# A fused spectral filter and gated FFN: one norm placed first on VectorE, five constants on GpSimd, a fold scratch in another tile

## The chip, the cores and the metric

The kernel runs on one core of a Trainium2 chip. The metric is the device time of one execution in microseconds. Engines are named as in the profile: PE is TensorE (PEld its weight loads), DVE is VectorE, ACT is ScalarE, POOL is GpSimd, SP is SyncE, which here only issues transfers.

## The reference

```
xn = layernorm(x)                                     # over D, eps 1e-5
X  = rfft2(xn, axes=(S, D)) * (w_r + 1j * w_i)
s  = irfft2(X, s=(S, D)).astype(bfloat16)
h  = (gelu(xn @ w_gate) * (xn @ w_up)) @ w_down       # tanh form of gelu
out = x + s * silu(h)
```

x is [1, 2048, 640] in bfloat16; the filters are [2048, 321]; the FFN has 640 inputs and 1536 hidden columns.

## The kernel before

**Tiling.** The 2048 rows are dealt into 16 slabs of 128 rows (slab n1 holds the rows n1, n1 + 16, ...). X holds all of them, [128, 16, 640]. Four slabs make a group of the FFN: normalized rows are transposed into xnT[g] (640 columns in 5 chunks of 128, by 512 rows); 12 hidden tiles each take a gate product (5 matmuls into a bank psg), a gelu on ScalarE (ge, line 799), an up product (5 matmuls into a bank psu) and a product of the two on VectorE (uT, line 801), which empties the bank. There are two banks of each name. Then come 12 matmuls for each output half (line 820), and the silu (lines 825 to 829).

**The FFT.** Its two axes are done by matmuls with sine tables that the kernel makes itself: integer phases (vt, ft_v, vg), a mask on VectorE, sines on ScalarE, some by transposing transfers. The tables Tinv and Tfwd are built from vt in the scratch tile GEN; FT and FI from fv; MG and its turned forms N1 and N2 from vg. The row axis is prepared by folds: VectorE adds and subtracts mirrored column blocks of four slabs at once (fold_x, fold_a, fold_b, then fold_y, lines 471 to 521), nine instructions for a set of four slabs. Their results f and y feed the matmuls pz (slab_S1, line 549), ScalarE copies those out, pd follows (slab_D), and the spectrum goes through DRAM (ZDR) into the tile B2. Then come the filter product with W1 and W2 (line 644), the way back through DRAM (UDR), the inverse matmuls (pv, pd at line 559), and the final product with the silu and sum with x (lines 770 and 771, x read again by load_xt, line 700).

**Scratch for the folds.** fold_x, fold_a and fold_y write to a scratch that overlays ftm and vt in GEN (scratch, line 464). So the folds of slabs 0 to 3 have to come after the sine that reads vt (tinv_sin, line 343). W2 is loaded with w_i much later (w_minus, w_plus, w_twin with index 1) and holds nothing until then.

**What sets the order.** The order is written out by hand. `back` (line 861) lists pieces of the FFN in turn; behind piece s the items of `plan[s]` run, put there by `put`. Each engine executes its instructions in program order; semaphores hold it where a buffer or an operand isn't ready. The places around the change: the first entry of `back` (slab 0's gate and up tiles, with slab 1's norm, in two parts, and its transposes between them), place 1 (inv_rest: six VectorE instructions for the pair i_r and o_r, read by ft_v of index 9 at place 12), places 17 to 23 (statistics of slabs 8 to 12), places 24 to 27 (folds of slabs 0 to 3), places 28 to 33 (folds of 4 to 7, with mg_mask at 30). A norm needs three steps: statistics on VectorE (lines 179 and 185), a power on GpSimd (line 197, its result rst), and the scaling on VectorE (line 208).

Of the kernel before, what the change touches and what calls it, by code (L numbers as in the profile page):

```python
# [10 lines left out]
BF16 = mybir.dt.bfloat16  # L11
INT32 = mybir.dt.int32
ACT = mybir.ActivationFunctionType
ALU = mybir.AluOpType
P = 128
S = 2048
D = 640
# [15 lines left out]
def kernel(  # L33
# [40 lines left out]
    with tc.manual_schedule():  # L74
        build(nc, locals())


def build(nc, env):
    consts, big, wts, xg, work, psA, psB = (env[k] for k in ("consts", "big", "wts", "xg", "work", "psA", "psB"))
    ZDR, UDR, X, Wg, Wu, Wd, W1, W2 = (env[k] for k in ("ZDR", "UDR", "X", "Wg", "Wu", "Wd", "W1", "W2"))  # L80
    xv, outv, wgv, wuv = (env[k] for k in ("xv", "outv", "wgv", "wuv"))
# [63 lines left out]
    GEN = big.tile([P, NH * L // 2], INT32, tag="sB", name="GEN")  # L145
# [17 lines left out]
    def c1(name, dt=FP32):  # L163
        return consts.tile([P, 1], dt, name=name)
# [75 lines left out]
    scr = goff[0]  # L240
# [7 lines left out]
    def bits(name, fields):  # L248
        n = len(fields)
        ti = consts.tile([P, n], INT32, name=name + "i")  # L250
        tf = consts.tile([P, n], FP32, name=name)
        for k, (shift, mask) in enumerate(fields):
            nc.vector.tensor_scalar(out=ti[:, k:k + 1], in0=pint, scalar1=shift, scalar2=mask,
                                    op0=ALU.logical_shift_right, op1=ALU.bitwise_and)
        nc.vector.tensor_copy(out=tf, in_=ti)
        return [tf[:, k:k + 1] for k in range(n)]

    def affine(name, src, a, b):
        t = c1(name)
        nc.vector.tensor_scalar(out=t, in0=src, scalar1=float(a), scalar2=float(b), op0=ALU.mult, op1=ALU.add)  # L260
        return t

    kh_f, hi_f, s_f, h_f, pf, n1_f, z_f = bits(
        "pb", [(1, 31), (6, 1), (0, 31), (5, 1), (0, 127), (1, 15), (0, 1)])
# [4 lines left out]
    def fma(name, src, k, add, dt=FP32):  # L269
        t = c1(name, dt)  # L270
        nc.vector.scalar_tensor_tensor(out=t, in0=src, scalar=float(k), in1=add, op0=ALU.mult, op1=ALU.add)
        return t
# [8 lines left out]
    def times(name, src, k, by):  # L281
        t = c1(name)
        nc.vector.scalar_tensor_tensor(out=t, in0=src, scalar=k, in1=by, op0=ALU.mult, op1=ALU.mult)
        return t
# [29 lines left out]

    def inv_rest():
        cq, hk = kc
        l_s = affine("l_s", s_f, 2.0, 256.0)
        l_k = fma("l_k", h_f, 2.0, l_s)
        l_r = fma("l_r", times("lh", hk, 1.0, hi_f), 1.0, l_k)
        i_r = affine("i_r", l_r, 2.0, 0.0)  # L320
        o_r = fma("o_r", l_r, 1.0, cq)
        ab.append((i_r, o_r))

    fwd_consts()
# [136 lines left out]

    y0s = {}

    def scratch(o, n, w):
        return GEN[:, scr + o:scr + o + n * w // 2].bitcast(BF16).rearrange("p (s d) -> p s d", s=n)

    def slabs(n0, n):
        assert all(("n", n0 + k) in done for k in range(n))
        return X[:, n0:n0 + n, :]

    def fold_y(n0, n, k):
        xn = slabs(n0, n)
        t = scratch(2304, n, 256)
        if k == 0:
            nc.vector.tensor_tensor(out=t, in0=xn[:, :, 0:256], in1=xn[:, :, 256:512], op=ALU.add)
            return
        if k == 1:
            y = work.tile([P, 4, P], BF16, tag="y0", bufs=2, name="y0")
            for a in range(n):
                y0s[n0 + a] = y[:, a, :]  # L480
            y0s[n0, n] = y = y[:, 0:n, :]
            nc.vector.tensor_tensor(out=y, in0=t[:, :, 0:P], in1=t[:, :, P:256], op=ALU.add)
            return
        y = y0s[n0, n]
        nc.vector.tensor_tensor(out=y, in0=y, in1=xn[:, :, 512:640], op=ALU.add)

    def fold_x(n0, n, k):
        xn = slabs(n0, n)
        xp = scratch(0, n, D)

        def blocks(t):
            return t.rearrange("p s (t e) -> p s t e", e=64)

        def outer(t):
            return t.rearrange("p s (t b e) -> p t s b e", b=2, e=64)[:, 0:5:2]

        ref = blocks(xn)[:, :, 2:8:5, :]
        if k == 0:
            nc.vector.tensor_tensor(out=outer(xp), in0=outer(xn),
                                    in1=ref.unsqueeze(1).to_broadcast([P, 3, n, 2, 64]), op=ALU.subtract)  # L500
        else:
            nc.vector.tensor_tensor(out=blocks(xp)[:, :, 6:2:-3, :], in0=blocks(xn)[:, :, 6:2:-3, :], in1=ref,
                                    op=ALU.subtract)

    def fold_a(n0, n, k):
        xp, uvt = scratch(0, n, D), scratch(1280, n, 512)
        lo = xp[:, :, 0:384].rearrange("p s (t e) -> p s t e", e=192)[:, :, :, 0:P]
        hi = xp[:, :, 256:640].rearrange("p s (t e) -> p s t e", e=192)[:, :, :, 64:192]
        nc.vector.tensor_tensor(out=uvt[:, :, 256 * k:256 * k + 256].rearrange("p s (t e) -> p s t e", e=P),  # L509
                                in0=lo, in1=hi, op=(ALU.add, ALU.subtract)[k])  # L510

    def fold_b(n0, n, k):
        if k == 0:
            f = work.tile([P, 4, 512], BF16, tag="xf", bufs=2, name="f")
            for a in range(n):
                xf[n0 + a] = f[:, a, :]
            xf[n0, n] = f[:, 0:n, :]
        s4 = scratch(1280, n, 512).rearrange("p s (w d) -> p s w d", w=2)
        dm = xf[n0, n].rearrange("p k (g d) -> p k g d", g=4)
        gs, op = ((slice(0, 4, 3), ALU.add), (slice(1, 3), ALU.subtract))[k]  # L520
        nc.vector.tensor_tensor(out=dm[:, :, gs, :], in0=s4[:, :, :, 0:P], in1=s4[:, :, :, 255:127:-1], op=op)  # L521
# [178 lines left out]
    def load_xt(pair):  # L700
        t = work.tile([P, 4, 512], BF16, tag="xf", bufs=2, name="xt")
        t = t.rearrange("p a b -> p (a b)")[:, 0:2 * D].rearrange("p (a d) -> p a d", a=2)
        for a in range(2):
            xts[2 * pair + a] = t[:, a, :]
        nc.sync.dma_start(out=t, in_=xv[:, 2 * pair:2 * pair + 2, :])

    def slab_S1i(n1):
        V = st_c["V"][n1]
# [128 lines left out]
    GG, UU = ((0, 0), (1, 0), (2, 0)), ((0, 1), (1, 1), (2, 1))  # L837
# [11 lines left out]
    def slab_Tparts(n1):  # L849
# [3 lines left out]
        for (a, b), ev in zip(PARTS, evs[::-1] if n1 == 0 else evs):  # L853
            pt = psB.tile([P, 5, P], BF16, tag="b")
            for c in range(a, b):
# [2 lines left out]
        done.add(("T", n1))  # L858

    NP = 8  # L860
    back = [(run, (ffn_slab, 0, GG + UU[:1]), (norm_parts, 1), (vt_iota, 1), (ffn_slab, 0, UU[1:2]),
             (slab_Tparts, 1), (ffn_slab, 0, UU[2:]), (bn_half, 2, 0)),
            (run, (ffn_slab, 1, GG[:2]), (bn_half, 2, 1), (ffn_slab, 1, UU[:1] + GG[2:] + UU[1:2]), (bn_join, 2),
             (root, 2, 1), (ffn_slab, 1, UU[2:]), (norm, 2))]
# [12 lines left out]
    def put(s, *item):  # L877
        plan[s].append(item)

    back.insert(2, (run,))  # L880
    plan.append([])
    put(1, inv_rest)
    put(2, bn_half, 3, 0)
    put(3, bn_half, 3, 1)
# [33 lines left out]
    put(31, mg_sin)  # L918
    put(31, mg_build)
    for at, *items in (  # L920
            (17, (stats, 8)), (18, (stats, 9)), (20, (stats, 10)), (22, (stats, 11), (root, 8, 4)), (23, (stats, 12)),
            (24, (fold_x, 0, 4, 0), (fold_x, 0, 4, 1)), (25, (fold_a, 0, 4, 0), (fold_a, 0, 4, 1)),
            (26, (fold_b, 0, 4, 0), (fold_b, 0, 4, 1)), (27, (fold_y, 0, 4, 0), (fold_y, 0, 4, 1), (fold_y, 0, 4, 2)),
            (28, (fold_x, 4, 4, 0)), (29, (fold_x, 4, 4, 1)), (30, (fold_a, 4, 4, 0)),
            (31, (fold_a, 4, 4, 1), (fold_b, 4, 4, 0)), (32, (fold_b, 4, 4, 1), (fold_y, 4, 4, 0)),
            (33, (fold_y, 4, 4, 1), (fold_y, 4, 4, 2), (norm, 8)), (34, (norm, 9), (norm, 10), (norm, 11)),
            (35, (stats, 13)), (36, (stats, 14), (stats, 15)),
            (37, (root, 12, 4), (fold_x, 8, 4, 0), (fold_x, 8, 4, 1)), (38, (fold_a, 8, 4, 0)),
            (39, (fold_a, 8, 4, 1), (fold_b, 8, 4, 0)), (40, (fold_b, 8, 4, 1)),
            (41, (fold_y, 8, 4, 0), (fold_y, 8, 4, 1)), (42, (fold_y, 8, 4, 2), (norm, 12)),  # L930
            (43, (norm, 13), (norm, 14), (norm, 15)), (44, (fold_x, 12, 4, 0)),
            (45, (fold_x, 12, 4, 1), (fold_a, 12, 4, 0)), (46, (fold_a, 12, 4, 1)),
            (47, (fold_b, 12, 4, 0), (fold_b, 12, 4, 1)), (48, (fold_y, 12, 4, 0)),
            (49, (fold_y, 12, 4, 1), (fold_y, 12, 4, 2))):
        for it in items:
            put(at, *it)
# [31 lines left out]
    for i, at in enumerate((vs0 - 1, vs0, vs0 + 6, vs0 + 15, vs0 + 24)):  # L968
        put(at, gather, i)
    put(vs0 - 2, load_xt, 0)  # L970
    put(vs0 + 4, load_xt, 1)
    for i, (n0, n) in enumerate(DG):
        a = vs0 + 7 * i
        for k in range(n):
            put(a + (2 * k if n == 3 else 1), slab_S1i, n0 + k)
        d = a + 6 if n == 3 else a + 3
# [55 lines left out]
```

## Time and profile before

| what | value |
|---|---|
| median of 3 runs | 201.37 us (201.34 to 201.65) |
| profiled execution | 201.39 us |
| its span, first to last instruction | 199.6 us |
| mean granted TensorE clock | 0.997 |
| DMA | 32.43 MB, mean 163 GB/s |

The span and the busy times are those of the one profiled execution; 1.79 us of its time lie around the span. A row of a timeline has the start in us, the busy time in us, the engine, the line, the operation, out<-in with shapes, and the number of instructions merged into the row; a bracket gives the idle time of the engine before the row and what ended it. A row of several matmuls ends when the last one leaves the pipeline, about 0.165 us after the next row can start, so rows overlap. In a row of transfers come the count, the size and the time from issue to landing. Lines of the page that end in percentages by engine are the chain of work that ended last, followed back from the last instruction.

### The profile page before, as it was taken

What the parts mean: (1) busy time and instruction counts of PE and PEld (TensorE: products, weight loads), DVE (VectorE), ACT (ScalarE), POOL (GpSimd) and SP (SyncE); (2) the same over time, 40 slices, a digit from 0 to 9 for tenths busy, and PEclk for the clock granted to TensorE, in tenths of its full rate; (3) what the DMA queues carried; (4) which work ended last, traced back from release to release, by engine and by line L of the source; (5) the groups of instructions that cost most, each with busy time, mean ns of one, the idle gap of its engine ahead of it and who ended that gap; (6) DMA issues with size and microseconds to landing.
All of it is one profiled execution on the core that took longest, in us unless ns stands there. A gap on an engine that the chain in (4) does not pass through costs nothing.

```text
span 199.6 us, 4145 instructions
## 1 busy us (share of the span) xinstructions
PE 192.4 (96%) x1533; PEld 118.3 (59%) x1548; DVE 131.7 (66%) x321; ACT 124.3 (62%) x219; POOL 37.8 (19%) x63
## 2 busy tenths in 40 slices
PE   7899999999999999999999999999999999999993
PEld 4688854767555555576543333457765555557772
DVE  7787869999899832223666556433349786977673
ACT  4567657966976677634788687523474747376631
POOL 4317869989030110000000000000000000000000
PEclk9999999999999999999999999999999999999998
DMA  5999997364575693329972022359700416142521
GB/s 174 328 364 371 371 291 163 82 206 171 154 152 149 143 321 90 113 66 298 259 203 99 5 99 102 132 130 274 258 0 34 135 36 194 36 131 42 192 79 55
DMA packets 37044, 32.43 MB, mean 163 GB/s; under 512 B 13088, under 2 KB 34976, under 8 KB 36768
## 3 DMA queue, kind: packets, MB, share of 16 engines
q1 hardware_dynamic: 36928, 30.86, 52.7%
q0 software_dynamic: 96, 1.31, 1.7%
q8 instruction: 12, 0.20, 0.4%
q14 instruction: 8, 0.07, 0.1%
HBM read 19.03 MB, written 7.88 MB: 135 GB/s over the span
## 4 chain that ended last, share of the span: by engine, by line
PE 87%; DVE 5%; ACT 4%; issue 1%; DMA 1%; POOL 0%; DVEq 0%
PE psg L795 25%; PE psu L795 25%; PE psu L820 11%; PE psg L820 11%; PE pv L712 2%; PE pd L559 2%; PE pu L659 2%; PE pd L580 2%; PE pz L549 2%; PE px L632 2%; DMA X<-in_A_x_dram 1%; PE pd L563 1%; DVE GEN L509 1%; DVE f L521 1%; DVE st L179 1%
## 5 line engine op out<-in xcount | busy, mean ns | idle before, releaser
L795 PE MATMUL psg<-xnT,Wg 128*128 128x512 bf16 (+2 forms) x287 | 60.5, 338 | 1.0 <-ACT xnT L857 0.2
L795 PE MATMUL psu<-xnT,Wu 128*128 128x512 bf16 (+2 forms) x288 | 60.7, 339 | 0.5 <-issue 0.2
L801 DVE TENSOR_TENSOR uT<-psu,ge 128x512 bf16<-128x512 f32 (+2 forms) x59 | 34.5, 586 | 26.7 <-PE psu L795 22.8
L820 PEld LDWEIGHTS <-uT 128*128 128x128 bf16 x396 | 37.3, 98 | 14.0 <-issue 0.4
L799 ACT ACTIVATE ge<-psg 128x512 bf16<-128x512 f32 (+2 forms) x59 | 30.5, 517 | 23.0 <-PE psg L795 22.1
L795 PEld LDWEIGHTS <-Wu 128*128 128x128 bf16 x295 | 26.9, 98 | 24.1 <-issue 2.5
L795 PEld LDWEIGHTS <-Wg 128*128 128x128 bf16 x295 | 26.6, 98 | 21.2 <-issue 2.3
L820 PE MATMUL psg<-Wd,uT 128*128 128x320 bf16 (+1 forms) x204 | 30.7, 295 | 0.0
L820 PE MATMUL psu<-Wd,uT 128*128 128x320 bf16 (+1 forms) x192 | 28.7, 296 | 0.0
L644 DVE TENSOR_TENSOR X<-xs,W 128x972 bf16<-128x972 bf16 (+2 forms) x22 | 13.3, 649 | 10.2 <-ACT xs L640 9.2
L585 ACT CAST zd<-pd 128x660 bf16<-128x660 f32 x16 | 11.3, 707 | 9.6 <-PE pd L582 8.8
L714 ACT CAST W<-pv 128x640 bf16<-128x640 f32 x16 | 11.1, 696 | 5.0 <-PE pv L712 5.0
L179 DVE BATCH_NORM_STATS2 st<-X 128x6 f32<-128x320 bf16 x32 | 14.0, 477 | 0.2 <-DMA X<-in_A_x_dram 0.2
L737 ACT ACTIVATE W<-pd 128x960 bf16<-128x960 f32 (+2 forms) x14 | 10.1, 780 | 5.6 <-PE pd L563 5.5
L665 ACT CAST X<-pu 128x486 bf16<-128x486 f32 (+4 forms) x22 | 12.3, 558 | 0.3
L640 ACT CAST xs<-px 128x972 bf16<-128x972 f32 (+2 forms) x11 | 10.3, 937 | 2.9 <-PE px L632 2.9
L551 ACT CAST GEN<-pz 128x640 bf16<-128x640 f32 x16 | 11.2, 700 | 1.3 <-PE pz L549 1.3
L829 DVE SCALAR_TENSOR_TENSOR G<-th,psg 128x320 bf16<-128x320 f32 x8 | 3.9, 488 | 12.2 <-ACT th L828 12.2
L743 DVE TENSOR_TENSOR W<-W 128x960 bf16<-128x960 bf16 (+1 forms) x12 | 6.9, 599 | 3.9 <-ACT W L737 3.8
L770 DVE TENSOR_TENSOR Yall<-Yall,G 128x640 bf16<-128x640 bf16 (+3 forms) x19 | 8.3, 435 | 1.6 <-ACT G L825 1.3
L771 DVE TENSOR_TENSOR Yall<-Yall,xt 128x640 bf16<-128x640 bf16 (+3 forms) x19 | 8.3, 439 | 0.7
L197 POOL TENSOR_TENSOR rst<-ve,mhalf 128x1 f32<-128x1 f32 (+1 forms) x6 | 5.6, 929 | 14.7 <-DVE ve L195 14.7
(139 smaller groups left out, 208.4 us busy)
## 6 DMA issues: line engine op xcount, KB each, us to landing
ZDR<-zd SPq DMA_DIRECT2D x32, 80.2 KB, 2.6
xt<-in_A_x_dram SPq DMA_DIRECT2D x8, 320.0 KB, 3.7
UDR<-X SPq DMA_DIRECT2D x10, 240.8 KB, 2.4
out_dram<-Yall SPq DMA_DIRECT2D x14, 160.0 KB, 2.1
B<-ZDR SPq DMA_DIRECT2D x8, 240.8 KB, 4.2
W<-UDR SPq DMA_DIRECT2D x4, 481.5 KB, 6.7
X<-in_A_x_dram SPq DMA_DIRECT2D x3, 640.0 KB, 10.8
Wd<-in_B_w_down_dram SPq DMA_DIRECT2D x1, 1920.0 KB, 14.2
```

Of the source, the lines that this page charges most:

```text
L179: nc.vector.bn_stats(out=st_n[n1][:, k, :], in_=X[:, n1, 320 * k:320 * k + 320])
L551: nc.scalar.copy(out=Zt[n1], in_=pz)
L585: nc.scalar.copy(out=zd.rearrange("p c (q e) -> p c q e", e=10), in_=pd[:, :, 0:330].rearrange("p c (e q) -> p c q e", q=33))
L640: nc.scalar.copy(out=xs, in_=px[:, :, 0:n * w].rearrange("p k (h l) -> p k h l", l=w))
L644: nc.vector.tensor_tensor(out=pp[-1], in0=xs, in1=WT[:, :, h0:h0 + n, l0:l0 + w], op=ALU.mult)
L665: nc.scalar.copy(out=us[:, :, :, c0:c0 + (w + 1 - m) // 2], in_=pv[:, :, :, m:w:2])
L714: nc.scalar.copy(out=vs, in_=pv)
L737: nc.scalar.activation(out=eo[:, b, :, a0:a1].rearrange("p k a n -> p a k n"), in_=py[b][:, a0:a1], func=ACT.Copy, scale=(2.0 if silu[a0] ...
L795: nc.tensor.matmul(ps, lhsT=WT[:, c, t * P:(t + 1) * P], rhs=xnT[g][:, c, c0:c1_], start=(c == 0), stop=(c == 4))
L799: nc.scalar.activation(out=ges[t], in_=ps, func=ACT.Gelu_apprx_tanh)
L801: nc.vector.tensor_tensor(out=uT[g][:, t, c0:c1_], in0=ps, in1=ges[t], op=ALU.mult)
L820: nc.tensor.matmul(ph, lhsT=uT[g][:, t, j * P:(j + 1) * P], rhs=Wd[:, t, c0:c1_], start=(t == 0), stop=(t == NT - 1))
```

## The change

It does five things. In the first entry of `back`, slab 1's norm (two VectorE instructions, and the small memset ahead of an iota) moves from behind slab 0's first up tile to ahead of it in program order; TensorE's order is the same, and on VectorE the norm now precedes the first two products uT. The constants of inv_rest are made by five instructions on GpSimd (one multiplies by hi_f and adds in one step) in place of six on VectorE; they stand on GpSimd between the powers of slabs 2 and 3. The scratch of the folds of slabs 0 to 3 lies in W2. The statistics of slabs 8 to 12 are put at places 16, 17, 18, 20 and 22 instead of 17, 18, 20, 22 and 23; on VectorE those of slabs 8 and 12 now precede a uT product that they followed. The loads of x for pairs 0 and 1 are issued one slab at a time.

```diff
     def inv_rest():
         cq, hk = kc
-        l_s = affine("l_s", s_f, 2.0, 256.0)
-        l_k = fma("l_k", h_f, 2.0, l_s)
-        l_r = fma("l_r", times("lh", hk, 1.0, hi_f), 1.0, l_k)
-        i_r = affine("i_r", l_r, 2.0, 0.0)
-        o_r = fma("o_r", l_r, 1.0, cq)
+        l_s, l_k, l_r, i_r, o_r = (c1(n) for n in ("l_s", "l_k", "l_r", "i_r", "o_r"))
+        for out, in0, s1, s2 in ((l_s, s_f, 2.0, 256.0), (l_k, h_f, 2.0, l_s), (l_r, hk, hi_f, l_k),
+                                 (i_r, l_r, 2.0, 0.0), (o_r, l_r, 1.0, cq)):
+            nc.gpsimd.tensor_scalar(out=out, in0=in0, scalar1=s1, scalar2=s2, op0=ALU.mult, op1=ALU.add)
         ab.append((i_r, o_r))
...
-    def scratch(o, n, w):
-        return GEN[:, scr + o:scr + o + n * w // 2].bitcast(BF16).rearrange("p (s d) -> p s d", s=n)
+    def scratch(n0, o, n, w):
+        if n0 == 0:
+            t = W2.rearrange("p a h l -> p (a h l)")[:, 2 * o:2 * o + n * w]
+        else:
+            t = GEN[:, scr + o:scr + o + n * w // 2].bitcast(BF16)
+        return t.rearrange("p (s d) -> p s d", s=n)
...
-        nc.sync.dma_start(out=t, in_=xv[:, 2 * pair:2 * pair + 2, :])
+        w = 1 if pair < 2 else 2
+        for a in range(0, 2, w):
+            nc.sync.dma_start(out=t[:, a:a + w, :], in_=xv[:, 2 * pair + a:2 * pair + a + w, :])
...
-    back = [(run, (ffn_slab, 0, GG + UU[:1]), (norm_parts, 1), (vt_iota, 1), (ffn_slab, 0, UU[1:2]),
+    back = [(run, (ffn_slab, 0, GG), (norm_parts, 1), (vt_iota, 1), (ffn_slab, 0, UU[:2]),
              (slab_Tparts, 1), (ffn_slab, 0, UU[2:]), (bn_half, 2, 0)),
...
-            (17, (stats, 8)), (18, (stats, 9)), (20, (stats, 10)), (22, (stats, 11), (root, 8, 4)), (23, (stats, 12)),
+            (16, (stats, 8)), (17, (stats, 9)), (18, (stats, 10)), (20, (stats, 11), (root, 8, 4)), (22, (stats, 12)),
```

The calls of scratch in fold_x, fold_a, fold_b and fold_y pass n0 as well.

## The prediction

> **What bounds the kernel now.** I read the page first: its busy line, then the chain of work that ended last, then the timelines of TensorE, VectorE, GpSimd and ScalarE around the edits.
>
> ```profile
> PE 192.4 (96%) x1533; PEld 118.3 (59%) x1548; DVE 131.7 (66%) x321; ACT 124.3 (62%) x219; POOL 37.8 (19%) x63
> PE 87%; DVE 5%; ACT 4%; issue 1%; DMA 1%; POOL 0%; DVEq 0%
> ```
>
> TensorE is busy for 96% of the span, and the change adds and removes no matmul: in the built kernels its instructions stand in the same order. So the time moves only by TensorE's idle stretches. I take the start of a group plus the number of its matmuls times their pitch (0.054 us for 128 columns, 0.109 for 256, 0.216 for 512, 0.136 for 320, all start to start in the timeline) and compare it with the start of the next. From 9.3 us on the groups touch, apart from a few tenths here and there (some, as at 58.2 us, are only a missing record). The stretches that an edit can reach are these:
>
> ```profile
> 7.20 0.72 PE L795 MATMUL psu<-xnT,Wu 128*128 128x128 bf16 x10
> 8.39 0.54 PE L856 MATMUL pt<-ident,X 128*128 128x128 bf16 x5 [0.47 <-DVE X L208]
> ...
> 13.49 0.71 PE L795 MATMUL psg<-xnT,Wg 128*128 128x256 bf16 x5
> 14.29 0.71 PE L795 MATMUL psu<-xnT,Wu 128*128 128x256 bf16 x5
> 14.84 0.71 PE L795 MATMUL psg<-xnT,Wg 128*128 128x256 bf16 x5
> 15.47 0.71 PE L795 MATMUL psu<-xnT,Wu 128*128 128x256 bf16 x5
> 16.24 0.45 PE L537 MATMUL pt<-ident,X 128*128 128x128 bf16 x5
> ```
>
> Idle: 7.75 to 8.39 (0.64, slab 1's norm), 9.04 to 9.30 (0.26, copies of slab 1's transposes), 14.04 to 14.29 (0.25) and 15.39 to 15.47 (0.08), both for a bank that VectorE empties late, and 16.02 to 16.24 (0.22, slab 3's norm). A last one lies at 42.82 to 43.11 (0.29): the matmul of the first y waits for the last fold.
>
> **Part 1, slab 1's norm ahead of two evictions.**
>
> ```profile
> 6.98 0.58 POOL L197 TENSOR_TENSOR rst<-ve,mhalf 128x1 f32<-128x1 f32 x1 [3.09 <-DVE ve L195]
> ...
> 7.76 0.29 DVE L801 TENSOR_TENSOR uT<-psu,ge 128x128 bf16<-128x128 f32 x1 [0.86 <-ACT ge L799]
> 7.96 0.63 DVE L208 TENSOR_SCALAR X<-X,mva,rst 128x384 bf16<-128x384 bf16 x2
> ```
>
> The factor is ready at 7.56, but VectorE sits on the eviction of the first up tile until 7.76, and the norm starts at 7.96. With the norm first it starts 0.04 behind the factor (so far apart are 12.25 and 12.29 at slab 2), at 7.60: 0.36 sooner. The two evictions follow at 8.16 and 8.36 instead of 7.76 and 8.52. Behind them the third up piece waits for a bank, free at 8.45 plus 0.04; the transposes end at 8.41, so that wait is 0.08, but it is hidden: the next matmuls wait anyway for slab 1's copies. ScalarE's moves from 8.77 to 8.41 with the transposes; VectorE's can start at 8.61 (it started at 8.97) since the second eviction leaves it at 8.56. Both end 0.36 sooner. **Gain 0.36**, and 9.30 becomes 8.94.
>
> **Part 2, five constants from VectorE to GpSimd.** VectorE spends 12.65 to 13.43 on six small instructions (l_s to o_r), 0.78, ahead of a half statistic and the eviction of 13.83. Everything there moves 0.36 with part 1; without the six the eviction starts at 12.69 (norm of slab 2 at 11.93, 0.36 to the half statistic, 0.40 to the eviction), 1.14 sooner. Its bank is free at 13.14, and TensorE comes for it at 13.68: the 0.25 goes, and so the 0.08 (next bank free at 14.3, wanted at 14.77). Slab 3's factor is asked for at 14.04 (15.15 less 1.11 to 1.14), the norm runs 14.62 to 15.07 and its transposes can start at 15.13. TensorE, 0.69 ahead by now, arrives at 15.34, so the 0.22 goes too. **Gain 0.55.** What is late next: the weights. The row for the third up block says 7.9 us from an issue at 5.54, so it lands at 13.44, and TensorE now wants it at 13.68: 0.24 of cover.
>
> ```profile
> Wu<-in_B_w_up_dram SPq DMA_DIRECT2D x1, 480.0 KB, 7.9
> ```
>
> GpSimd's five constants are new, and stand between the factors of slabs 2 and 3. The nearest rows are its scalar instructions of 128x1 between 33.61 and 36.21: ten starts in 2.60 us, 0.26 each; with waits on one another up to 0.35. That is 1.3 to 1.75 us behind 11.89, over at 13.2 to 13.6; the factor is asked for at 14.04. The largest row of that shape (46.39, beside folds) has 0.62: 3.1 us, done at 14.99, 0.95 late, less 0.21 of cover at the transposes: 0.74 lost. The low end is nothing, since the constants are not read before 23 us. I take nothing, because the rows beside statistics and evictions are the nearest to what VectorE does there.
>
> **Part 3, statistics of slabs 8 to 12 sooner, folds of 0 to 3 in another tile.**
>
> ```profile
> 36.12 2.17 ACT L345 ACTIVATE Tinv<-GEN,negpi 128x1024 bf16<-128x1024 int32 x2
> ...
> 37.36 0.96 DVE L499 TENSOR_TENSOR GEN<-X 128x1536 bf16<-128x1536 bf16 x1 [0.16 <-ACT Tinv L345]
> ...
> 42.59 0.46 DVE L485 TENSOR_TENSOR y<-y,X 128x512 bf16<-128x512 bf16 x1
> ```
>
> The folds overwrite the phases that the sine reads, so they wait for it; they take 5.70, and y is ready at 43.06. In W2 they wait for VectorE alone. I ran its new order forward with all starts 0.91 sooner: eviction 8 at 28.45 (its gelu ends then), statistics 9 and 10, eviction 9 at 31.1, statistic 11, eviction 10 at 32.9, statistic 12, eviction 11 at 34.58 to 35.25, folds 35.2 to 40.9. TensorE wants y at 41.9, so 1.0 is spare: **gain 0.29**. The statistics read loads that landed at 21.4 and 29.2, before their new places (26.7 and 33.5). Eviction 11 is now behind statistic 12; its reader is the twelfth matmul of the first down group, at 35.57, so 0.3 remains. The loads of w_i into W2 now wait for the folds: SyncE issues the first at 47.96, less 1.2, long after 40.9. Nothing is queued up there.
>
> Folds 4 to 7 stay in the old tile; the sine is done at 37.4 and they start at 40.8, so they don't wait. But the mask of vg, third on VectorE among them, waits for GpSimd's eight vg steps:
>
> ```profile
> 37.06 0.37 POOL L384 TENSOR_SCALAR vg<-kr,n1x,phm 128x16 int32<-128x16 int32 x1
> 37.40 1.42 POOL L384 TENSOR_SCALAR vg<-kr,n1x,phs 128x16 int32<-128x16 int32 x1
> ```
>
> Such a step takes 0.37 until the folds begin and 1.42 beside the first of them. Now all eight, from 35.5 on, meet folds. VectorE reaches the mask at 42.0; by then at least four are done, and with VectorE waiting the rest take 0.37 to 0.5 each, so the mask ends at 43.0 to 44.2. ScalarE wants it at 43.24 and has nothing else until 44.36 (0.72 idle before 45.55 in its timeline), the instruction itself 0.40. Cost 0 to 0.3; I take 0, as folds of 4 to 7 have 5 us until their matmul at 53.06. The Trainium skill ("SBUF — State Buffer", section "SBUF: two separate sides") says that a VectorE instruction with two SBUF inputs and a GpSimd instruction lock a shared port pair for a whole instruction, the later one fully blocked. The trace agrees (0.37 against 1.42); by that rule this edit costs GpSimd some 4 us more beside folds, and the sum stays, or loses the 0.3.
>
> **The xt loads** of pairs 0 and 1 become four issues instead of two, 0.4 us more each on SyncE's queue, which is idle from 139.4 to 152.88; first read at about 150. Nothing.
>
> **Sum.** 0.36 + 0.55 + 0.29 = 1.20. The profiled execution took 201.39 (span 199.6 and 1.79 around it), 0.02 above the median of 201.37. 201.39 - 1.20 = 200.19; I predict **200.2**. Behind 43 us TensorE has the same work in the same order and its suppliers move with it.
>
> **The rivals.** (a) The forecast, 0.60, itself between 200.0 and 200.4. (b) The weights become the bound in the head: with a landing some 0.5 later than the row, the 0.24 of cover is gone and 0.3 lost, 200.5. For it: the loads run at 358 GB/s through that stretch; against: the row itself. 0.12. (c) The last fold still ends late or the mask holds ScalarE: the 0.29 stays, 200.5; against it 1.0 of cover. 0.10. (d) Slower: GpSimd's constants. One mechanism, between the factors of slabs 2 and 3. Free for the five are 14.04 + 0.21 - 11.89 = 2.36 us, 0.47 each. Above 3.56, 0.71 each, the gain is eaten; at 1.42 each (vg beside folds) they take 7.1, slab 3's transposes wait 4.7, and 204.9 results. For it: factor and norm wait in GpSimd's order; against: no two-input fold runs there. 0.08, with the milder 0.74 loss (200.9) at its edge. (e) The change does not do what it says: TensorE finds the banks and copies just as late through another wait, 201.4. The idle stretches have VectorE's rows right ahead of them, so 0.10.
>
> **Numbers.** A measurement here can tell about 0.2%, 0.4 us. Faster by more (below 200.97): a, b, c, 0.82; within: e, 0.10; slower: d, 0.08. Range 199.8 to 201.0: it holds a to c with the bound of the constants (200.9), and 0.2 below the lowest term for what I may not have seen.
>
> **What would show it.** Right: the norm of slab 1 starts at 7.6 and slab 1's first gate matmul near 8.95; no idle on TensorE at its fifth up tile or slab 3's transposes, which start near 15.3; y's matmul directly behind its f group, folds from 35.2. Wrong: a weight load of Wu ending later than TensorE's arrival at 13.7, five long GpSimd rows behind 11.9, a ScalarE wait for the mask near 43.5, or new idle behind 50 us.

## The result, and the profile after

The changed kernel takes **201.04 us** (median of 9 runs, 200.58 to 201.59) against 201.47 (9 runs, 201.34 to 201.72) for the kernel before in the same measurement: a ratio of 0.9976 with a 95% interval from 0.9965 to 0.9987. It is faster, by 0.43 us and not by the 1.2 that were forecast, and lies just outside the range. The profiled execution took 201.11 (span 199.3), against 201.39 (199.6).

So there are two questions: did the terms of the sum come, and if so, where did they go? First the stretches of TensorE that the prediction named, in the timeline of the changed kernel:

```profile
7.40 0.72 PE L800 MATMUL psu<-xnT,Wu 128*128 128x128 bf16 x10
8.39 0.54 PE L861 MATMUL pt<-ident,X 128*128 128x128 bf16 x5 [0.26 <-DVE X L208]
8.85 0.44 PE L800 MATMUL psu<-xnT,Wu 128*128 128x128 bf16 x5
9.30 0.72 PE L800 MATMUL psg<-xnT,Wg 128*128 128x128 bf16 x10
...
13.49 0.71 PE L800 MATMUL psg<-xnT,Wg 128*128 128x256 bf16 x5
14.03 0.71 PE L800 MATMUL psu<-xnT,Wu 128*128 128x256 bf16 x5
14.58 0.71 PE L800 MATMUL psg<-xnT,Wg 128*128 128x256 bf16 x5
15.12 0.71 PE L800 MATMUL psu<-xnT,Wu 128*128 128x256 bf16 x5
15.67 0.44 PE L540 MATMUL pt<-ident,X 128*128 128x128 bf16 x5
```

From 13.49 to 15.67 each group starts 0.54 or 0.55 behind the one before, which is its own length: the idle stretches of before (0.25, 0.08, 0.22) are gone. At 8.39 a wait for slab 1's norm is still there (0.26 instead of 0.47), and slab 1's first gate matmul starts at 9.30, as before, not at 8.94. The first y follows its f group at once:

```profile
42.01 0.39 PE L552 MATMUL pz<-Tfwd,f 128*128 128x128 bf16 x4
42.24 0.22 PE L552 MATMUL pz<-Tfwd,y 128*128 128x128 bf16 x1
```

The lead lasts. TensorE's last group of the down product starts at 194.44, against 195.31 in before, and VectorE's last instruction ends at 196.11, against 196.97: 0.86 sooner. But the span is only 0.3 shorter. From VectorE's last end to the end of the span before took 2.63 and the changed kernel takes 3.19. I call this stretch **the tail**; the spans are printed to 0.1, so a tail is good to some 0.05. These are VectorE's last instruction and SyncE's last issue, first before, then after:

```profile
196.74 0.23 DVE L771 TENSOR_TENSOR Yall<-Yall,xt 128x128 bf16<-128x128 bf16 x1
197.00 0.33 SPq L772 DMA_DIRECT2D out_dram<-Yall  x1
```

```profile
195.88 0.23 DVE L776 TENSOR_TENSOR Yall<-Yall,xt 128x128 bf16<-128x128 bf16 x1
196.35 0.33 SPq L777 DMA_DIRECT2D out_dram<-Yall  x1
```

Before, the last output transfer is issued 0.03 behind VectorE's end; after, 0.24 behind. And it takes longer to land. The DMA view from 195.5 to 198.8 (one slice of the GB/s line is 0.0825 us; an issue shows its size and the time to landing), before and then after:

```profile
GB/s 0 0 0 0 0 0 0 0 0 0 0 0 93 256 365 225 55 0 0 0 0 61 223 242 70 0 0 0 96 208 90 3 0 0 99 0 0 0 0 0
q14 instruction: 1, 0.01, 0.8%
out_dram<-Yall SPq DMA_DIRECT2D x1, 32.0 KB, 1.4
```

```profile
GB/s 0 8 186 295 264 202 39 0 0 0 0 140 284 154 19 0 0 99 0 0 65 183 112 13 16 9 0 0 0 0 0 0 0 0 0 0 0 0 0 0
q14 instruction: 1, 0.01, 1.1%
out_dram<-Yall SPq DMA_DIRECT2D x1, 32.0 KB, 2.0
```

The bursts are output transfers. The single slice of 99 GB/s is something else: one packet of 8 KB (99 GB/s times 0.0825 us) on the queue q14, kind "instruction". Before, it passes at 198.3, behind the data of the last transfer. After, it passes at 196.9, behind the issue but ahead of that data, whose end then trickles (13, 16, 9), and the landing is 2.0 behind the issue instead of 1.4. By the trace's own records the issue loses 0.21 and the landing 0.53, together 0.75 of the 0.86: the last landing is at 198.32, against 198.43 before. The span is 0.25 shorter because the stretch from the last landing to its end, in which SyncE closes the program, is shorter too (1.02 against 1.15). At its end SyncE waits 1.2 for the output instead of 0.4 (the waits of its queue, after):

```profile
SPq L1032 <- DMA out_dram<-Yall: 1.2, 1, 1.2
```

### The profile page after: what moved, and what is told of

It is laid out like the page before. It is cut to its first block, busy times and chain, and to the rows that moved or that the text cites. A ratio compares the mean times of both kernels' runs of the same rounds, so it can differ in the third digit from the quotient of the medians.

```text
span 199.3 us, 4162 instructions
## 1 busy us (share of the span) xinstructions
PE 193.7 (97%) x1548; PEld 119.1 (60%) x1548; DVE 130.9 (66%) x315; ACT 124.5 (62%) x219; POOL 39.8 (20%) x68
## 4 chain that ended last, share of the span: by engine, by line
PE 95%; DVE 1%; ACT 1%; POOL 0%; issue 0%
PE psu L800 26%; PE psg L800 26%; PE psg L825 13%; PE psu L825 13%; PE pv L717 2%; PE pd L562 2%; PE pu L662 2%; PE pz L552 2%; PE psg L599 2%; PE pd L583 2%; PE px L635 2%; PE pd L566 1%; PE pt L861 1%; PE pd L585 0%; DVE st L179 0%; ACT G L830 0%
## 5 line engine op out<-in xcount | busy, mean ns | idle before, releaser
L800 PE MATMUL psg<-xnT,Wg 128*128 128x512 bf16 (+2 forms) x295 | 61.5, 340 | 0.1
L800 PE MATMUL psu<-xnT,Wu 128*128 128x512 bf16 (+2 forms) x295 | 61.4, 340 | 0.0
```

What stands on the lines that cost most here:

```text
L800: nc.tensor.matmul(ps, lhsT=WT[:, c, t * P:(t + 1) * P], rhs=xnT[g][:, c, c0:c1_], start=(c == 0), stop=(c == 4))
```

## The experiments

The theories at this point were: the terms came as forecast and the end gave half of them back, because SyncE has two more issues (the split xt loads); or the terms are smaller than they look in one profile; or the end varies from execution to execution and means nothing. Where a label says "merged", the last two pairs of loads into B2 are one pair, which takes two issues from SyncE's program and leaves the work of the other engines as it was. All ratios are against the kernel before as measured together with the run.

| run | median us | before us | ratio and 95% interval | tail us | SyncE instructions |
|---|---|---|---|---|---|
| the change | 201.04 | 201.47 | 0.9976 (0.9965 to 0.9987) | 3.19 | 224 |
| e1 change without split | 201.36 | 201.39 | 0.9991 (0.9979 to 1.0003) | 3.42 | 223 |
| e2 split alone | 202.04 | 201.39 | 1.0032 (1.0018 to 1.0046) | 3.26 | 223 |
| e3 norm alone | 201.16 | 201.39 | 0.9984 (0.9972 to 0.9995) | 2.65 | 222 |
| e4 constants alone | 200.77 | 201.39 | 0.9970 (0.9954 to 0.9986) | 2.66 | 222 |
| f1 change, merged | 200.39 | 201.47 | 0.9948 (0.9936 to 0.9960) | 2.61 | 222 |
| f3 change without split, merged | 200.53 | 201.47 | 0.9951 (0.9939 to 0.9963) | 2.72 | 221 |
| f4 folds and statistics alone, merged | 201.27 | 201.47 | 0.9997 (0.9986 to 1.0008) | 2.77 | 221 |
| f5 before, merged | 201.89 | 201.47 | 1.0025 (1.0016 to 1.0034) | 3.06 | 220 |
| g1 before, 2 more on SyncE | 201.99 | 201.41 | 1.0026 (1.0017 to 1.0035) | 3.27 | 224 |
| g2 change, 30 more on SyncE | 200.24 | 201.41 | 0.9935 (0.9923 to 0.9946) | 2.48 | 254 |
| g3 as f1, norm back | 200.64 | 201.41 | 0.9958 (0.9946 to 0.9970) | 2.59 | 222 |
| h1 before, 30 more on SyncE | 201.35 | 201.30 | 0.9998 (0.9989 to 1.0007) | 2.60 | 252 |

The tail is from the profiled execution; the last column counts SyncE's instructions in the built kernel (before has 222, tail 2.63). Differences below are between medians.

### The split, away and alone

e1 undoes the split in the changed kernel, e2 makes it in the kernel before.

```diff
-        w = 1 if pair < 2 else 2
-        for a in range(0, 2, w):
-            nc.sync.dma_start(out=t[:, a:a + w, :], in_=xv[:, 2 * pair + a:2 * pair + a + w, :])
+        nc.sync.dma_start(out=t, in_=xv[:, 2 * pair:2 * pair + 2, :])
```

> The change without the split of the xt loads (pairs 0 and 1 loaded in one transfer each, as before). Tail theory (the two added transfers make the last output transfer end later, by about 0.6 us): this is 0.4 to 0.6 us faster than the change, near 200.5, and its last transfer is issued 0.03 us behind VectorE's last instruction and lands in 1.4 us. Rival, the ends only scatter from execution to execution: the same time as the change within 0.2 us, 201.0, with the same spread of about 1 us.

> The kernel before with only the split of the xt loads. Tail theory: slower than before by 0.4 to 0.6 us, near 202.0. Rival (the split costs nothing, the ends scatter): the time of before within 0.2 us, 201.5.

e2 is 0.65 slower than before, with a tail of 3.26: two issues that sit in idle time at 150 us, and a loss in the last 3 us. So far the split. But e1, without it, is not faster than the change, it is 0.32 slower, and its tail is 3.42. **The split is enough to lengthen the end, but it is not what does it in the changed kernel**; that form of the theory falls. What both have in common with the change is the count: 223, 223 and 224, against 222. In e1 the one more is the added wait of the w_i loads for the folds in W2 (73 semaphore records on SyncE against 72 in before).

### The norm and the constants alone

e3 is the kernel before with one line of the change, e4 with the five constants on GpSimd alone.

```diff
-    back = [(run, (ffn_slab, 0, GG + UU[:1]), (norm_parts, 1), (vt_iota, 1), (ffn_slab, 0, UU[1:2]),
+    back = [(run, (ffn_slab, 0, GG), (norm_parts, 1), (vt_iota, 1), (ffn_slab, 0, UU[:2]),
```

> The kernel before with only slab 1's norm ahead of the two evictions. Terms theory (the idle removed in the head is worth 0.36 us whenever the first load comes at the same time): faster by 0.36, 201.1; the norm starts 0.04 us behind the factor and slab 1's first gate matmul comes near 8.95, later only by as much as slab 0's first statistic starts behind 3.0. Rival, a floor in the head (that matmul stays at 9.3 whatever the norm does, since slab 0's own start slips): the same time as before, 201.5.

> The kernel before with only the five constants on GpSimd. Terms theory: TensorE loses its waits of 0.25, 0.08 and 0.22 us at 14.0 to 16.2 us, 0.55 faster, 200.9. Rival, scatter or a later wait gives it back: TensorE's waits are gone but the time is within 0.2 us of before.

The norm alone brings 0.23, the constants alone 0.62. Both leave SyncE's 222 instructions alone, and their tails are those of before (2.65 and 2.66), so the medians show the terms without the end. e4's TensorE has no idle from 13.75 on:

```profile
13.75 0.71 PE L794 MATMUL psg<-xnT,Wg 128*128 128x256 bf16 x5
14.30 0.71 PE L794 MATMUL psu<-xnT,Wu 128*128 128x256 bf16 x5
14.85 0.71 PE L794 MATMUL psg<-xnT,Wg 128*128 128x256 bf16 x5
15.39 0.71 PE L794 MATMUL psu<-xnT,Wu 128*128 128x256 bf16 x5
15.94 0.44 PE L536 MATMUL pt<-ident,X 128*128 128x128 bf16 x5
```

### SyncE's count brought back: the merged loads

If the count decides, then taking two instructions away anywhere should give the end back. f1, f3 and f4 do it in the change, in the change without the split, and in the kernel before with the folds and statistics of the change; f5 is the control, the merge alone in the kernel before.

```diff
-        for h0, h1 in ((0, 3), (3, 6), (6, 9), (9, 12), (12, 16)):
+        for h0, h1 in ((0, 3), (3, 6), (6, 9), (9, 16)):
```

> The change with the last two of the five pairs of B2 loads (parts 9 to 12 and 12 to 16) issued as one pair: two transfers fewer on SyncE, whose program is 222 instructions long as before (the change: 224; the change without the split and the split alone: 223 each; before, norm alone and constants alone: 222). Program-length theory (past 222 SyncE has to fetch a last piece of program right before the last output transfer, and the end comes 0.55 to 0.8 us later): 0.55 faster than the change, 200.5, with the end 2.65 us behind VectorE's last instruction instead of 3.19. Rival, the end hangs on VectorE's folds or the split itself: still 3.2 behind and 201.0.

> The change without the split of the xt loads and with the same merged B2 loads; 221 SyncE instructions. Program-length theory: 0.6 to 0.8 faster than the change without the split (201.36), 200.6, end 2.65 behind VectorE's last instruction. Rival: as the change without the split, 201.4.

> The kernel before with only the folds of 0 to 3 in W2 and the statistics of 8 to 12 sooner, and the merged B2 loads; 221 SyncE instructions. Terms theory: the wait for y (0.17 to 0.29 us in the traces) is gone and nothing else moves, faster than before by 0.2 to 0.3, 201.15. Rival, the earlier folds cost something later: same as before or slower.

> The kernel before with only the merged B2 loads, a control; 220 SyncE instructions. Program-length theory: no gain, since before is already short enough, 201.4 within 0.1. Rival (the merged loads themselves save time): faster by about 0.5.

f1 is 0.65 faster than the change, f3 0.83 faster than e1, and both have the short tail again. f4 gives the size of the third term, 0.20 in the medians; its interval reaches past 1, so it is only known to be small. Its tail is 0.14 longer than that of before (2.77 against 2.63), so without its end the term may be up to 0.34; that rests on one profile of each. In its timeline the y follows its f group at once (42.77 behind 42.55).

The control missed: f5 should have been as before and is 0.42 slower. Its last transfer is issued at once (197.07, VectorE ends at 197.04) and lands in 1.4, yet its tail is 3.06. So fewer instructions aren't simply better; there is a place to hit. Two marks show which. One is the packet of q14, in the DMA view of each run in steps of 0.2 us. The other is in the trace's records of SyncE's own instructions, of which the timeline shows the issues alone; the records begin behind the first four, so before has 218 of its 222. In every run SyncE stands still for 0.35 to 0.46 us between its 207th and its 208th recorded instruction:

| SyncE instructions | runs | where SyncE stands still, and for how long, us | packet behind VectorE's end, us | tail, us |
|---|---|---|---|---|
| 223 and 224 | the change, e1, e2, g1 | ahead of the last issue, 0.35 to 0.36 | 0.7 to 0.9 | 3.19 to 3.42 |
| 222 | before, e3, e4, f1, g3 | between the last issue and its landing, 0.35 to 0.37 | 1.2 to 1.3 | 2.59 to 2.66 |
| 221 | f3, f4 | the same, 0.46 (the wait for the landing ends with it) | 2.0 | 2.72, 2.77 |
| 220 | f5 | behind the last landing, 0.36 | 2.4 | 3.06 |
| 252 and 254 | h1, g2 | at 165.7 and 162.9 us, 0.38 and 0.37 | none from 194 us on | 2.60, 2.48 |

The column of the packet counts from VectorE's end to the start of the step. In 12 of the runs the packet starts 0.99 to 1.02 behind the end of the 207th instruction (1.29 and 2.02 in h1 and g2). A second such stop, of 0.44 to 0.45, stands in all 14 runs ahead of the 80th recorded instruction, 128 earlier, with a packet of its own 1.1 to 1.5 behind. So stop and packet come at fixed places of SyncE's program, as the fetch of a further piece of it would: with fewer instructions ahead of the end they come later against it. SyncE goes on some 0.6 before the packet starts, so the stop is not a wait for that packet.

At 223 and 224 the two do separate harm. The stop lies across VectorE's last end and holds the issue for 0.2. The packet, which starts 0.6 behind the issue, meets the data: one sixteenth of the transfer (nine of its 144 packets, the small closing ones included) starts only when the instruction packet ends, at 197.50 in the change and within 0.01 of that end in e1, e2 and g1 too. The landing of this sixteenth comes 0.3 to 0.6 behind the other fifteen (198.32 and 197.85 in the change). Its packets, alone in the DMA view of the change from 197.48 to 197.64:

```profile
q1 hardware_dynamic: 9, 0.00, 6.0%
```

At 220 the stop stands behind the last landing (198.51), where nothing covers it. From the last landing to the end of the span f5 takes 1.64 against 1.15 in before; of the 0.49 more, 0.36 is the stop, and the rest lies in two further semaphore records of SyncE that before has behind it by the time of its landing. The packet itself, at 199.55, costs f5 nothing: the last step of the program, across which it passes, takes 0.56 as in before.

### The count alone

The last runs change nothing but the count: drains on SyncE's queue behind the loads of x at the start, where there is nothing to drain but SyncE's own order.

```diff
+    for _ in range(30):
+        nc.sync.drain()
```

g1 puts two of them into the kernel before (224 instructions, as the change has); g2 puts 30 into the change, and h1, its control, 30 into the kernel before.

> The kernel before with two drains on SyncE behind its first loads: no transfer, wait or engine's work changes, SyncE's program is 224 instructions instead of 222. Program-length theory: the end comes 0.5 to 0.8 us later, 202.0, with TensorE as before. Rival (the late end belongs to the changed transfers or folds): 201.45 as before.

> The change as it is, with 30 drains on SyncE behind its first loads (254 instructions, most of which pass while SyncE has nothing else to issue). Program-length theory (only the place of the fetch counts, not the length as such): the fetch now falls some 30 instructions ahead of the last transfer, where SyncE is idle; the end is back at 2.65 behind VectorE's last instruction and the time near 200.5, 0.55 faster than the change although more is executed. Rival (more instructions cost more, or the split and the folds are what costs): 201.0 or above.

> The kernel before with the same 30 drains on SyncE (252 instructions), the control for the change with 30 drains (200.24). Program-length theory: before had an even end already, so nothing is gained or lost, 201.4, and the change is worth about 1.17 us against it. Rival (the drains help by themselves, by holding back the w_r loads for instance): faster than 201.2.

g1 does no other work than the kernel before and is 0.58 slower. VectorE ends at 197.03, only 0.06 later than before, and the end looks like that of the change: the issue 0.25 behind VectorE's end, the packet of q14 0.6 behind the issue, the landing late (timeline, then the DMA view from 197.2 to 198.0 and its issue):

```profile
196.81 0.22 DVE L774 TENSOR_TENSOR Yall<-Yall,xt 128x128 bf16<-128x128 bf16 x1
197.28 0.33 SPq L775 DMA_DIRECT2D out_dram<-Yall  x1
```

```profile
q14 instruction: 1, 0.01, 3.9%
out_dram<-Yall SPq DMA_DIRECT2D x1, 32.0 KB, 1.8
```

g2 is the best of all, **200.24**, 0.80 faster than the change. Its packet passes between 164.6 and 165.2, in the middle of other work, and none does at the end (timeline; then the DMA view from 195.5 to 198.8, where q1 is the only queue):

```profile
195.80 0.22 DVE L779 TENSOR_TENSOR Yall<-Yall,xt 128x128 bf16<-128x128 bf16 x1
196.05 0.33 SPq L780 DMA_DIRECT2D out_dram<-Yall  x1
```

```profile
GB/s 8 178 303 264 194 47 0 0 0 0 149 270 154 23 0 0 22 174 165 38 0 0 0 0 0 0 0 0 0 0 0 0 0 0 0 0 0 0 0 0
q1 hardware_dynamic: 432, 0.16, 19.2%
out_dram<-Yall SPq DMA_DIRECT2D x1, 32.0 KB, 1.4
```

The last burst is whole again (22, 174, 165, 38, nothing behind it), 0.02 from VectorE's end to the issue, 1.4 to the landing. h1 shows that the drains as such do nothing: 201.35 against 201.30. With the end out of the way, the change is worth 201.47 - 200.39 = 1.08 by f1, which has the 222 instructions of before, and 201.41 - 200.24 = 1.17 by g2, of which 0.12 may be a shorter closing (1.03 from the last landing to the end, against 1.15 in h1 and before).

### The norm once more

g3 is f1 with the norm back behind the first up tile, so that the norm's term is measured in the surroundings of the change as well.

> The change with merged B2 loads (222 SyncE instructions) and slab 1's norm back behind the first eviction. It tells what the norm is worth once the end is even. Full-term theory: 0.36 slower than 200.39, 200.75. Rival (in executions whose dummy matmuls run at half rate until past 5 us the factor itself comes late, so the norm gains only about 0.25): 200.64.

It takes 200.64, f1 took 200.39: 0.25, as in e3 (0.23).

## Why the prediction was wrong, point by point

**What bounds the kernel: right.** Idle time taken from TensorE at 9, 14 and 43 us arrived at VectorE's last instruction at 196 (0.86 in the profile of the change). Nothing behind 43 us ate it on the way.

**The norm, 0.36: right in kind, 0.23 to 0.25 in size.** The norm starts 0.03 behind its factor, as forecast (7.34 + 0.58, then 7.95):

```profile
7.34 0.58 POOL L197 TENSOR_TENSOR rst<-ve,mhalf 128x1 f32<-128x1 f32 x1 [3.44 <-DVE ve L195]
7.95 0.64 DVE L208 TENSOR_SCALAR X<-X,mva,rst 128x384 bf16<-128x384 bf16 x2 [0.70 <-POOL rst L197]
```

But the factor itself is 0.36 later than in before (6.98), and that moves from profile to profile: its instruction starts at 7.22 in f5, 7.04 in g3, 7.24 in e3, 7.44 in f1. What the edit takes away is the distance from the factor to the end of the eviction; both ends move. The norm starts 0.31 behind the factor's end in f5 (8.11 behind 7.80), 0.40 in before, 0.66 in g3 (8.28 behind 7.62), 0.15 in f4; the mean over the eight profiles without the edit is 0.33, and with the edit 0.03 stay. I read one execution and took its distance for a constant. In the change's profile the factor is so late that 9.30 stayed 9.30. Why it is late is not shown: its instruction starts at 7.20 or later in all ten profiles with a long slow start of TensorE (last section) and at 7.08 or sooner in before, e2 and g3 with a short one, but at 7.37 in e4, where the slow start is short as well.

**The constants, 0.55: right**, 0.62 by the medians. On GpSimd they run from 12.23 to 13.84, 1.6 us, inside the 1.3 to 1.75 of the estimate, and GpSimd is idle for 0.54 before it is asked for the next factor. That was rival (d), slower through GpSimd; it did not occur:

```profile
12.23 0.19 POOL L320 TENSOR_SCALAR l_s<-pb 128x1 f32<-128x1 f32 x1
...
13.57 0.27 POOL L320 TENSOR_SCALAR o_r<-l_r,cq 128x1 f32<-128x1 f32 x1
14.38 0.55 POOL L197 TENSOR_TENSOR rst<-ve,mhalf 128x1 f32<-128x1 f32 x1 [0.54 <-DVE ve L195]
```

**The folds, 0.29: right in kind**, 0.20 by the medians of f4 and up to 0.34 without its longer end, though the interval of f4 holds zero too. They run from 35.51 to 41.06 (forecast 35.2 to 40.9). Rival (c), the late mask, did not occur: the mask ends at 43.60, within the forecast 43.0 to 44.2, and ScalarE, busy with another instruction until then, takes it at 43.63.

```profile
38.29 1.88 POOL L383 TENSOR_SCALAR vg<-kr,n1x,phm 128x16 int32<-128x16 int32 x1
...
42.30 0.36 POOL L383 TENSOR_SCALAR vg<-kr,n1x,phs 128x16 int32<-128x16 int32 x1
...
43.37 0.23 DVE L422 TENSOR_SCALAR vg<-vg 128x128 int32<-128x128 int32 x1 [1.12 <-POOL vg L383]
```

Five of the eight vg steps met folds and took 0.54 to 1.88, the three behind them 0.36: some 4 us more, hidden, as the prediction had it.

**Rivals (b) and (e)** did not occur either: no group of the changed kernel's head waits for weights, and each of the named waits is gone or shorter.

**The step that failed** is the last one before the sum: "The xt loads of pairs 0 and 1 become four issues instead of two ... Nothing", and with it the wait that the w_i loads got, "Nothing is queued up there". Each was priced by the time it takes where it stands, and there it is indeed free. But together they make SyncE's program two instructions longer, and that moves its stop at the 208th recorded instruction from behind the last output issue to just ahead of it, and the packet that follows from behind the transfer's data to ahead of it. Two empty instructions alone cost 0.58 (g1), the split alone 0.65 (e2); without their effect the change takes 200.39 (f1) or 200.24 (g2). The sum then stands: 0.25 + 0.62 + 0.20 = 1.07 by parts, 1.08 to 1.17 as a whole, against 1.20 forecast; less 0.65 to 0.80 for the end, it comes to about the 0.43 that was measured. No rival had this mechanism; the page of before showed the queue (12 + 8 packets of kind "instruction"), and I did not ask when its packets pass. That the sum came out near the whole is in part luck: the norm was taken too large and the constants too small.

The Trainium skill ("Runtime: NRT & Kernel Launch", section "Instruction fetch mechanics") says that an engine's instruction memory is refilled in blocks of 256 instructions by the sequencer's own DMA queue while the program runs, and that crossing into a new block is mostly hidden. The runs agree on a fetch at fixed places in the program, over a queue of kind "instruction", and on the cover in the middle (164.6 to 165.2 in g2, no cost). They differ in the size, 128 instructions from one stop to the next and 8 KB in each packet on SyncE, and at the end of the kernel, where it costs 0.6 to 0.8; the measurement decides.

## What to carry to other kernels

A term read from an idle stretch holds if the stretch is the difference of two paths that keep their distance; check that in several executions before you take it for a constant. And an instruction that is free where it stands still lengthens its engine's program: on the engine that issues the last output, look in the profile after each edit at when the last "instruction" packet passes, and if it meets the last transfer, move it with empty instructions early in the program (30 here). Compare edits only between kernels whose ends are alike, or an effect of 0.6 us at the end hides a gain of 1.1.

## What the runs showed of the hardware

- **The place of an instruction fetch is worth 0.6 to 0.8 us here.** SyncE stops for 0.35 to 0.46 ahead of its 208th recorded instruction in all 14 runs, and an 8 KB packet follows. Where the stop falls ahead of the last issue, the issue is 0.2 late, and one sixteenth of that transfer of 32 KB waits for the packet's end; it lands 1.8 to 2.1 behind the issue (g1, the change, e2 and e1), against 1.4 in before, f1 and g2. Part of this is open: the last landing comes 0.63 to 0.70 behind the last data there, against 0.34 to 0.35 in the other runs, and what holds it is not shown.
- **TensorE's first matmuls run at half rate for a time that differs between executions.** The 18 dummy matmuls before the first transposes took 3.46 in e2, 3.51 in the profile of before, 3.64 in e4, 3.88 in g3 and 4.02 in all others; in the change's profile the slow rate lasts into slab 0's transposes (0.71 for five instead of 0.54). A dummy matmul follows the one before by 0.213 in this state and a matmul of the same shape by 0.109 later; 4.02 means that all 18 were slow. The page's line of the granted clock shows full speed all along, but only because it counts time without a record as full: the trace's first clock record starts at 3.91 us (e2), 4.02 (before), 6.42 (the change) or 6.72 (f5), within 0.2 of where the rate doubles. So the granted clock fits as the cause; what sets the moment is open. With it the head of the kernel differs from execution to execution, with no edit.

```profile
1.18 4.02 PE L599 MATMUL psg<-GEN 128*128 128x256 bf16 x18 [1.18 <-DVE eps L219]
5.13 0.71 PE L861 MATMUL pt<-ident,X 128*128 128x128 bf16 x5
```
